# Early parking of x, a wider gate and 36 readerless products in an attention-and-mixer kernel

## The chip, the cores and the metric

The kernel runs on one core of a Trainium2 chip. The metric is the time of one execution on the device, in microseconds; runs of the kernel before have the median 647.34 us (three runs, 647.22 to 649.98).

## The reference

```python
# 4 batches, 8 heads, 768 tokens, head dim 64; chunks of 32 tokens see 16 tokens
# to the left, 8 to the right and 8 memory tokens
scores = scale * np.matmul(q_c, k_full.transpose(0, 1, 3, 2))
a = np.exp(scores - np.max(scores, axis=-1, keepdims=True))
out[:, :, c_start:c_end] = np.matmul(a / (a.sum(-1, keepdims=True) + 1e-9), v_full)
...
x = out.transpose(0, 2, 1, 3).reshape(B, S, H * D)      # 4 x 768 x 512
u = x + (x.transpose(0, 2, 1) @ U @ V).transpose(0, 2, 1)  # U 768x32, V 32x768
return u + np.maximum(u @ w_ch1, 0.0) @ w_ch2            # w1 512x2048, w2 2048x512
```

q, k, v and the memory tokens are float32. U, V, w1 and w2 are float64 in DRAM; the kernel reads them as pairs of 32-bit integers.

## The kernel before

A batch has six x tiles of 128 tokens x 512; three of them make a block (TB = 3), two make an attention step T (0 to 2). Attention of a step: q and k are transposed on TensorE (L582, out of qn and kn) and copied out by ACT (qt, L642); L661 makes the scores; DVE takes maximum and difference (`softmax_`, L697, L698), ACT the exponential (L704); pt is transposed (L760), copied by ACT (L763) and multiplied with v (L790); DVE multiplies by the reciprocal sums and so writes x (L804).

The mixer: the float64 words are put together by `Words` in four steps, begin (L216, ACT), bits (L223, L224, DVE), low (L230, ACT) and join (L237, DVE). U and V are decoded once, each piece of w1 and w2 once, for batch 0. Products with float32 accuracy are made as three, out of high and low halves (names ending in h and l). u = x + ... is made transposed (uh, ul, L1099, L1100), hidden units in pieces f = 0 to 15 of 128 (`w1_step`, L1159, then ACT's relu hh, L1165, and DVE's hl, L1166) and `w2_step` adds them up in PSUM (L1213, L1218), after a first product with v3 and the gate tile g (L1199). `add_to_x` (L1174) adds the sums to x.

Batch 0 is done in `both_blocks`: 32 units n; units 0 to 17 alternate block 0 and block 1 for f = 0 to 8, units 18 to 24 are block 0 with f = 9 to 15, units 25 to 31 the same of block 1. Batches 1 to 3 are done in `fast`, where the weights enter through sums of quarter matrices: GpSimd makes these sums (`prepare`, L1346), DVE and ACT the turned folds tl and th (L1394, L1393). In `prepare` for p = 1 GpSimd first copies one element of tl to a tile named gate_ (L1334), so that its sums start behind that part of the fold.

x tiles live in a pool of 19 buffers ("slot") that weights in raw form, temporaries and x share. `put_by` notes that an x tile is to go to DRAM, `let_go` issues the noted stores on ACT's queue (L1144), `recall` loads x back on SP's queue (L1149).

Order: the program is written engine by engine. SP's queue, the loads of q, k, v (L563: v; vbe is the third of the three v tiles, for T = 2), U, V and weights (rw and raw, L316 and L326) among it, keeps the order of the code throughout; TensorE and GpSimd too; DVE to unit 18; ACT to unit 2 (`head.close()`), and behind that a scheduler sets the order, which may also move an instruction ahead of earlier ones. DVE's one-element memset of rw (L315) makes SP's first weight load wait for DVE's place.

`keep_clock(n)` counts products of the zero tile `busy` (128x512, bf16) that `att_ps` issues ahead of the next bank's work, without a reader. FILL gives the counts for six places; the first two have 2 each, the others none.

Of the kernel before, what the change touches and what calls it, by code (L numbers as in the profile page):

```python
# [9 lines left out]
F32 = mybir.dt.float32  # L10
F32R = mybir.dt.float32r
BF16 = mybir.dt.bfloat16
# [15 lines left out]
HEAD = {ET.Activation}  # L28
FIRST = 3000
START = 90  # L30
FILL = [2, 2, 0, 0, 0, 0]
BANKS = (
    "o0 o1 h h a a a h h a a o0 o1 a a h h o0 o1 a a h h o0 o1 a a o0 o1 a h h a a o0 a a"
)
# [2 lines left out]
HIGH = 400  # L37
LEAD = 0
LATE = 0
SPLIT = 9  # L40
# [15 lines left out]
def chunk_attn_then_mixer_kernel(  # L56
# [13 lines left out]
    nc = tc.nc  # L70
    ctx.enter_context(tc.manual_schedule(engines={mybir.EngineType.SP}))
    P = 128
# [16 lines left out]
    TB = 3  # L89
    NBLK = NT // TB  # L90
    TOK = TB * P
# [51 lines left out]
    def keep_clock(n, m=0):  # L143
        warm[0] += n
        small[0] += m

    busy = slot([P, 512], BF16, "busy")
    nc.vector.memset(busy, 0.0)
# [20 lines left out]
    for j in range(4):  # L169
        nc.gpsimd.tensor_copy(  # L170
            out=rep[32 * j:32 * j + 32],
# [966 lines left out]
    def put_by(b, t):  # L1138
        held.append((x_d[b, t], xs.pop((b, t))))

    def let_go(eng=nc.scalar):
        while held:
            to, x = held.pop(0)
            eng.dma_start(out=to, in_=x)  # L1144
# [25 lines left out]

    def add_to_x(b, t, bank, last):
        x = xs[(b, t)]
        with tc.high_priority(offset=2 * HIGH if last else 0):
            nc.vector.tensor_tensor(out=x, in0=bank, in1=x, op=ALU.add)  # L1174
        if last:
            held.append((out[b, t * P:(t + 1) * P, :], xs.pop((b, t))))
            if b == B - 1 or b == 0 and t >= TB:
                let_go(nc.sync)
        else:
            put_by(b, t)  # L1180
# [3 lines left out]
    def w2_step(b, blk, f, where, begins, ends, hh, hl):  # L1184

        if begins:
            for tt in range(TB):
                if where == 1 or where == 2 and tt == 2:
                    accs[where, tt] = ps_b.tile([P, 512], F32, name="ps_a", tag="bank")
                elif where == 2:  # L1190
                    accs[where, tt] = ps_b.tile([P, 512], F32, name="ps_h", tag="bank")
                else:
                    accs[where, tt] = ps_o.tile([P, CH], F32, name=f"acc{tt}")
        acc = [accs[where, tt] for tt in range(TB)]
        if begins and f == 0 and b == 0:
            begins = False
            for tt in range(TB):
                t = blk * TB + tt
                nc.tensor.matmul(out=acc[tt], lhsT=v3[:, t * P:(t + 1) * P], rhs=gate[0], start=True, stop=False)  # L1199
        passes = [(hh, w2h[f]), (hh, w2l[f]), (hl, w2h[f])]  # L1200
        if ends is not None and b >= CLASSIC:
            for tt in range(TB):
                sl = slice(tt * P, (tt + 1) * P)
                for m, (h, w) in enumerate(passes):
                    nc.tensor.matmul(  # L1205
                        out=acc[tt], lhsT=h[:, sl], rhs=w, start=False, stop=(m == 2),
                    )
                add_to_x(b, blk * TB + tt, acc[tt], ends)
            return
        for tt in range(TB):  # L1210
            sl = slice(tt * P, (tt + 1) * P)
            for m, (h, w) in enumerate(passes[:2]):
                nc.tensor.matmul(  # L1213
                    out=acc[tt], lhsT=h[:, sl], rhs=w, start=(begins and m == 0), stop=False,
                )
        for tt in range(TB):
            sl = slice(tt * P, (tt + 1) * P)
            nc.tensor.matmul(out=acc[tt], lhsT=hl[:, sl], rhs=w2h[f], start=False, stop=ends is not None)  # L1218
        if ends is not None:
            for tt in range(TB):  # L1220
                add_to_x(b, blk * TB + tt, acc[tt], ends)
# [5 lines left out]
    def both_blocks(following):  # L1227

        units = []
        for f in range(SPLIT + LEAD):  # L1230
            if f < SPLIT:
                units.append((0, f, 0, f == 0, None))
            if f >= LEAD:
                g = f - LEAD
                units.append((1, g, 1, g == 0, False if g == SPLIT - 1 else None))
        units += [(0, f, 0, False, True if f == NF - 1 else None) for f in range(SPLIT, NF)]
        units += [(1, f, 0, f == SPLIT, True if f == NF - 1 else None) for f in range(SPLIT, NF)]
        prev = []
        for n, (blk, f, where, begins, ends) in enumerate(units):
            while done[0] < min(2 * NF, 2 * f + 1 + (n > LATE)):  # L1240
                advance(1)
                more_w()
            if n == 2:
                head.close()
            let_go()
            solo = n >= 2 * SPLIT
            if n == 2 * SPLIT:
                paced.close()
            for blk_, m, *_ in units[n:n + AHEAD + 1]:
                if m >= SPLIT and blk_ == 1:  # L1250
                    get_w1l(m)
            w1l = w1ls[f]
            if f >= SPLIT or blk == 1:
                del w1ls[f]
            if n == 2 * SPLIT - SOON:
                place(1)
            serve(RATEL if n < 2 * SPLIT else RATES)
            if n > 2 * SPLIT:
                border()
            if n == 0:  # L1260
                for c, g3 in rest[:2]:
                    join_uT1(turn_x1(c), c, g3)
            if n == len(units) - 1:
                for m in range(3):
                    build_factor(0, m)
            hid_ = w1_step(0, blk, f, w1l)
            if n == len(units) - 5:
                open_turned()
            if n == len(units) - 1:
                open_fast()  # L1270
            if n == 0:
                decode(2, 4)
                for c, g3 in rest[2:]:
                    join_uT1(turn_x1(c), c, g3)
                decode(1, 1)
                decode(2, 6)
                decode(1, 6)
                decode(3, 2)
            for _ in range(RATE + (3 < n < 12)):
                advance(1)  # L1280
                more_w()
            if n > 2 * SPLIT:
                border()
            if n == len(units) - 3:
                prepare(0, True)
            if n >= len(units) - 3:
                following()
            if n == len(units) - 1:
                recall(0, 1)
                for m in (3, 4):  # L1290
                    build_factor(0, m)
            prev.append((blk, f, where, begins, ends) + hid_)
            if solo or n % 2 == 0 or ends:
                while len(prev) > (not ends):
                    while done[0] < 2 * prev[0][1] + 2:
                        advance(1)
                        more_w()
                    w2_step(0, *prev.pop(0))
# [21 lines left out]
        place(PLAN[at[0]])  # L1320
        at[0] += 1

    gate_ = const.tile([P, 1], F32, name="gate")
    sums_d = [[dram.tile([P, 2, 2, P], F32, name=f"sumsd{p}_{m}") for m in range(3)] for p in range(NF // 2)]

    def prepare(p, first):

        if first:
            whole = [slot([P, NCK, P], F32, "val") for _ in range(2)]
            for side in range(2):  # L1330
                nc.gpsimd.dma_start(out=whole[side], in_=val_d[2 * p + side])
            mixed[p, 1], mixed[p, 3] = whole[1][:, 2:4, :], whole[0][:, 0:2, :]
            if p == 1:
                nc.gpsimd.tensor_copy(out=gate_[0:1], in_=turned[0][1][0:1, 4, 0, TOK - 1:TOK].bitcast(F32))  # L1334
        else:
            plain = slot([P, 2, 2, P], F32, "plain")
        for m, (n, fa, ca, fb, cb, op) in enumerate(SUMS):
            if m % 2 == 0:
                two = slot([P, 2, 2, P], F32, "sums")
                used = slice(0, 1 if m + 1 == len(SUMS) else 2)  # L1340
                if not first:
                    nc.sync.dma_start(out=two[:, used], in_=sums_d[p][m // 2][:, used])
            mixed[p, n] = two[:, m % 2]
            if first:
                a, b_ = (whole[f][:, 2 * c:2 * c + 2, :] for f, c in ((fa, ca), (fb, cb)))
                nc.gpsimd.tensor_tensor(out=two[:, m % 2], in0=a, in1=b_, op=getattr(ALU, op))  # L1346
                if m % 2 == 1 or m + 1 == len(SUMS):
                    summed.append((p, sums_d[p][m // 2][:, used], two[:, used]))
            elif m == 0:
                for n, side in ((1, 1), (3, 0)):  # L1350
                    mixed[p, n] = plain[:, side]
                    nc.sync.dma_start(out=plain[:, side], in_=val_d[2 * p + side][:, 2 * side:2 * side + 2])
# [244 lines left out]
```

## Time and profile before

| | |
|---|---|
| median of the runs shown | 647.34 us (647.22, 647.34, 649.98) |
| the profiled execution's own time | 647.76 us |
| its span in the profile | 646.0 us |
| granted TensorE clock, mean over the span | 0.993 of full speed |
| TensorE, DVE, ACT, GpSimd busy | 626.6, 422.4, 306.6, 75.0 us |
| chain that ended last | 88% TensorE, 4% DVE, 2% SP's queue, 2% ACT, 2% DMA |

The span is what the profiler sees, from the first to the last instruction; the execution's own time has the launch around it. Times in the rows are microseconds from the span's start. "[0.86 <-ACT dec L230]" at a row's end says that the engine was idle that long before the row's first instruction, and what ended it. Instructions of one line are merged in the timelines (x4: four of them; start and total time). Queue rows (SPq, ACTq) show the issue of a transfer, not the transfer.

### The profile page before, as it was taken

How to read it: one execution, taken by the hardware profiler on the slowest of the kernel's cores; microseconds unless marked ns; L12 is line 12 of the kernel's file. 1: busy time of each engine (PE TensorE's matmuls, PEld its weight loads, DVE VectorE, ACT ScalarE, POOL GpSimd, SP SyncE). 2: the span in 40 equal slices, each digit the busy share in tenths (PEclk: the TensorE clock that was granted, in tenths of full speed). 3: DMA queues.
4: the chain of work that ended last, by engine and by line, in shares of the span. 5: the costliest groups of instructions: out<-in, count | busy, mean ns of one | idle time of the engine just before them, and what ended most of it. 6: DMA issues, size and time to landing. Idle time of an engine off the chain costs nothing.

```text
span 646.0 us, 15746 instructions
## 1 busy us (share of the span) xinstructions
PE 626.6 (97%) x6196; PEld 548.8 (85%) x6198; DVE 422.4 (65%) x889; ACT 306.6 (47%) x770; POOL 75.0 (12%) x129
## 2 busy tenths in 40 slices
PE   7798999999999999989999999999999999999997
PEld 6567999988879899879898899888888899889986
DVE  4977997887529867449676864556666974427442
ACT  4666776685316454524344555633333653315320
POOL 3710011100120642123300000000000000000000
PEclk9999999999999999989999999999999999999999
DMA  9998695696606689414371699144532662100021
GB/s 206 192 306 294 212 261 180 181 255 177 185 22 220 183 219 208 132 35 157 100 236 52 170 208 230 43 116 124 148 114 82 189 221 90 50 34 16 2 79 69
DMA packets 134357, 96.83 MB, mean 150 GB/s; under 512 B 88842, under 2 KB 111114, under 8 KB 134282
## 3 DMA queue, kind: packets, MB, share of 16 engines
q1 hardware_dynamic: 121690, 70.25, 41.2%
q10 hardware_dynamic: 9936, 17.04, 7.2%
q0 software_dynamic: 2656, 8.52, 3.8%
q8 instruction: 49, 0.80, 0.5%
q14 instruction: 26, 0.21, 0.1%
HBM read 69.44 MB, written 25.43 MB: 147 GB/s over the span
## 4 chain that ended last, share of the span: by engine, by line
PE 88%; DVE 4%; SPq 2%; ACT 2%; DMA 2%; issue 1%; DVEq 0%; ACTq 0%
PE ps_h L1459 19%; PE acc L1213 14%; PE ps_h L1159 10%; PE ps_a L1459 8%; PE acc L1218 7%; PE ps_h L1213 6%; PE ps_a L1213 5%; PE ps_h L1218 3%; PE ps_a L582 2%; PE ps_a L1218 2%; PE ps_a L790 2%; PE ps_a L661 2%; PE ps_h L1205 1%; PE ps_a L760 1%; PE ps_a L1379 1%
## 5 line engine op out<-in xcount | busy, mean ns | idle before, releaser
L1213 PE MATMUL acc<-w,hh 128*128 128x512 f32 x366 | 97.1, 400 | 0.9 <-DVE w L367 0.9
L1459 PE MATMUL ps_h<-th,w1l 128*128 128x384 f32 x288 | 83.3, 342 | 0.5 <-DVE part L1474 0.5
L1213 PEld LDWEIGHTS acc<-w,hh 128*128 128x128 f32 x366 | 66.9, 188 | 15.2 <-issue 1.5
L1435 DVE SCALAR_TENSOR_TENSOR hl<-kept,hh 128x384 fp32r<-128x384 f32 x48 | 26.7, 556 | 50.9 <-PE ps_a L1218 25.7
L1459 PEld LDWEIGHTS ps_h<-th,w1l 128*128 128x128 f32 x288 | 52.8, 187 | 3.7 <-issue 1.7
L1434 ACT ACTIVATE hh<-kept 128x384 fp32r<-128x384 f32 x48 | 25.5, 531 | 64.0 <-PE ps_a L1213 41.5
L1459 PE MATMUL ps_h<-th,s 128*128 128x384 f32 x192 | 53.0, 337 | 0.0
L1218 PE MATMUL acc<-w,hl 128*128 128x512 f32 x183 | 51.6, 390 | 0.0
L1459 PE MATMUL ps_h<-tl,w1l 128*128 128x384 f32 x144 | 48.5, 337 | 0.0
L1213 PE MATMUL ps_h<-w,hh 128*128 128x512 f32 x156 | 43.9, 404 | 1.8 <-issue 1.8
L1159 PE MATMUL ps_h<-uh,w1h 128*128 128x384 f32 x124 | 42.5, 348 | 0.7 <-ACT uh L1131 0.6
L1159 PE MATMUL ps_h<-ul,w1h 128*128 128x384 f32 x124 | 40.9, 337 | 0.0
L1218 PEld LDWEIGHTS acc<-w,hl 128*128 128x128 f32 x183 | 34.4, 188 | 7.4
L1213 PE MATMUL ps_a<-w,hh 128*128 128x512 f32 x132 | 38.1, 392 | 1.7 <-ACT hh L1165 1.7
L1465 ACT COPY part<-ps_h 128x384 f32<-128x384 f32 x24 | 11.5, 479 | 55.5 <-PE ps_h L1459 34.5
L1427 ACT CAST s<-sums 128x256 fp32r<-128x256 f32 x72 | 28.6, 411 | 16.3 <-PE ps_h L1459 16.1
L1213 PEld LDWEIGHTS ps_h<-w,hh 128*128 128x128 f32 x156 | 29.0, 192 | 7.8 <-issue 1.9
L1459 PEld LDWEIGHTS ps_h<-th,s 128*128 128x128 f32 x192 | 35.1, 188 | 0.2 <-DVE part L1469 0.2
L1346 POOL TENSOR_TENSOR sums<-val 128x256 f32<-128x256 f32 x40 | 31.9, 825 | 28.1 <-DMA val<-vald 11.0
L1459 PE MATMUL ps_h<-tl,s 128*128 128x384 f32 x96 | 32.3, 337 | 0.0
L1213 PEld LDWEIGHTS ps_a<-w,hh 128*128 128x128 f32 x132 | 25.0, 190 | 7.5 <-ACT hh L1165 2.2
L1428 DVE TENSOR_TENSOR s<-sums,s 128x256 fp32r<-128x256 f32 x72 | 30.4, 434 | 1.0 <-ACT s L1427 0.8
(280 smaller groups left out, 1393.8 us busy)
## 6 DMA issues: line engine op xcount, KB each, us to landing
sums<-sumsd SPq DMA_DIRECT2D x32, 256.0 KB
xd<-x ACTq DMA_DIRECT2D x30, 256.0 KB
x<-xd SPq DMA_DIRECT2D x30, 256.0 KB
rw<-in_moe_w_ch_dram SPq DMA_DIRECT2D x14, 512.0 KB
vb<-in_v_dram SPq DMA_DIRECT2D x56, 98.0 KB
raw<-in_moe_w_ch_dram SPq DMA_DIRECT2D x20, 256.0 KB
qn<-in_q_dram SPq DMA_DIRECT2D x36, 128.0 KB
rw<-in_moe_w_ch_dram SPq DMA_DIRECT2D x16, 256.0 KB
```

The source lines that it names most:

```text
L582: nc.tensor.transpose(out=psv[:, p, r, :], in_=half[:, r, 2 * p:2 * p + 2, :].rearrange("n h d -> n (h d)"), identity=ident,)
L661: nc.tensor.matmul(out=psv[s][CK * i:CK * i + CK, t, p % 2, p // 2, :], lhsT=qt[p // 2][rows, p % 2, NI * t + i, :], rhs=kall[rows, NB * ( ...
L790: nc.tensor.matmul(out=psv[g][CK * i:CK * i + CK, t, j], lhsT=pt[j % 2][rows, 2 * t + j // 2, CK * i:CK * i + CK], rhs=vt[rows, NI * t + i ...
L1159: nc.tensor.matmul(out=ph[:, :TOK], lhsT=w[:, c, :], rhs=u[c], start=(m == 0), stop=(m + 1 == len(parts)),)
L1213: nc.tensor.matmul(out=acc[tt], lhsT=h[:, sl], rhs=w, start=(begins and m == 0), stop=False,)
L1218: nc.tensor.matmul(out=acc[tt], lhsT=hl[:, sl], rhs=w2h[f], start=False, stop=ends is not None)
L1346: nc.gpsimd.tensor_tensor(out=two[:, m % 2], in0=a, in1=b_, op=getattr(ALU, op))
L1427: nc.scalar.copy(out=s[:, 0:2], in_=total)
L1428: nc.vector.tensor_tensor(out=s[:, 2:4], in0=total, in1=s[:, 0:2].bitcast(F32), op=ALU.subtract)
L1434: nc.scalar.activation(out=hh, in_=src, func=AF.Relu)
L1435: nc.vector.scalar_tensor_tensor(out=hl, in0=src, scalar=0.0, in1=hh.bitcast(F32), op0=ALU.max, op1=ALU.subtract,)
L1459: nc.tensor.matmul(out=banks[at_], lhsT=w[:, wc, :], rhs=t[:, i, c, :], start=(n < 3 and m == 0), stop=(m + 1 == len(parts)), skip_group_c ...
```

## The change

- FILL[3] goes from 0 to 6: six readerless products ahead of the transposes of the last q part (`keep_clock(FILL[3])`, L911).
- `fill`: 30 readerless 32x64 products out of ident into acc[0], ahead of the gate products (L1199) of block 1's first `w2_step`; none for block 0.
- At unit 2, behind `head.close()`, x of block 0 (three tiles of 256 KB) is put by, to DRAM; at unit 21 `recall(0, 0)` loads it.
- gate_ has seven columns: GpSimd's copy reads one element of all seven parts of tl, not of part 4 alone.
- In batch 0, the last add to x has a high priority only for block 0.

```diff
-FILL = [2, 2, 0, 0, 0, 0]
+FILL = [2, 2, 0, 6, 0, 0]
...
+    def fill(ps, n):
+
+        ones = ident.bitcast(BF16)
+        for _ in range(n):
+            nc.tensor.matmul(out=ps[0:32, 0:64], lhsT=ones[:, 0:32], rhs=ones[:, 0:64], start=True, stop=True)
...
     def add_to_x(b, t, bank, last):
         x = xs[(b, t)]
-        with tc.high_priority(offset=2 * HIGH if last else 0):
+        with tc.high_priority(offset=2 * HIGH if last and (b > 0 or t < TB) else 0):
...
         if begins and f == 0 and b == 0:
             begins = False
+            fill(acc[0], 30 * blk)
             for tt in range(TB):
...
             if n == 2:
                 head.close()
+                for t in range(TB):
+                    put_by(0, t)
+            if n == 2 * SPLIT + 3:
+                recall(0, 0)
             let_go()
...
-    gate_ = const.tile([P, 1], F32, name="gate")
+    gate_ = const.tile([P, 7], F32, name="gate")
...
             if p == 1:
-                nc.gpsimd.tensor_copy(out=gate_[0:1], in_=turned[0][1][0:1, 4, 0, TOK - 1:TOK].bitcast(F32))
+                nc.gpsimd.tensor_copy(out=gate_[0:1], in_=turned[0][1][0:1, :, 0, TOK - 1].bitcast(F32))
```

ACT's queue in the kernel before, at the q copies of T = 2 (dec is U and V in decoding, qt the copied q, v_96 the tile v3); what an instruction waits for stands in brackets, DMAHW0 to DMAHW7 are the completion counters that the DMAs of SP and ACT take in turn:

```order
L216 ACTIVATE dec_749<-vraw_108 96x256 [waits DMAHW4_49,DMAHW3_49,DMAHW5_49,DMAHW1_49,DVE_49]
L642 COPY qt_756<-ps_h_751 128x2x128 [waits PE_49]
L642 COPY qt_756<-ps_h_751 128x2x128
L642 COPY qt_764<-ps_h_759 128x2x128 [waits PE_49,Activation_49]
L642 COPY qt_764<-ps_h_759 128x2x128
L763 COPY pt_625<-acc0_775 128x512 [waits PE_49]
L763 COPY pt_649<-acc1_781 128x512 [waits PE_49]
L230 ACTIVATE dec_733<-uarea_107 128x192 [waits DVE_49,Activation_49]
L230 ACTIVATE dec_749<-vraw_108 96x256 [waits DVE_49,Activation_49]
L704 ACTIVATE pt_862<-pt_862 128x512 [waits DVE_49]
L704 ACTIVATE pt_868<-pt_868 128x512 [waits DVE_49]
L265 CAST v3_96<-ps_a_956 96x256 [waits PE_49]
```

The same place of ACT's queue in the changed kernel (its lines stand some six higher):

```order
L222 ACTIVATE dec_749<-vraw_108 96x256 [waits DMAHW4_49,DMAHW3_49,DMAHW5_49,DMAHW1_49,DVE_49]
L1150 DMA xd0_0_141<-x_773 128x512 [waits DMAHW0_49,DVE_49]
L648 COPY qt_762<-ps_h_751 128x2x128 [waits PE_49]
L648 COPY qt_762<-ps_h_751 128x2x128
L1150 DMA xd0_1_142<-x_776 128x512 [waits DMAHW1_49,DVE_49]
L648 COPY qt_770<-ps_h_765 128x2x128 [waits PE_49,Activation_49]
L648 COPY qt_770<-ps_h_765 128x2x128
L769 COPY pt_625<-acc0_781 128x512 [waits PE_49]
L769 COPY pt_649<-acc1_787 128x512 [waits PE_49]
L236 ACTIVATE dec_733<-uarea_107 128x192 [waits DVE_49,Activation_49]
L1150 DMA xd0_2_143<-x_956 128x512 [waits DMAHW1_49,DVE_49]
L271 CAST v3_96<-ps_a_962 96x256 [waits PE_49]
```

The three stores of x stand in ACT's front now, the first two between the decode of V and the second pair of q copies, the third ahead of the casts of v3; between L236 and the third store there are also the second L236 and the two exponentials, as before.

SP's queue in the changed kernel, the loads of vbe, and the first weight loads behind them (this piece of the queue has the same transfers in both kernels):

```order
L569 DMA vbe_101<-in_v_dram 56x7x64 [waits DMAHW6_49,Pool_49]
L569 DMA vbe_101<-in_v_dram 56x7x64 [waits DMAHW7_49]
L569 DMA vbe_101<-in_v_dram 56x7x64 [waits DMAHW0_49]
L569 DMA vbe_101<-in_v_dram 56x7x64 [waits DMAHW1_49]
L577 DMA vbe_101<-in_v_dram 48x4x64 [waits DMAHW2_49]
...
L322 DMA rw1_879<-in_moe_w_ch1_dram 128x2x256 [waits DMAHW2_49,DVE_49]
L322 DMA raw_882<-in_moe_w_ch1_dram 128x2x256 [waits DMAHW3_49]
L332 DMA rw2_884<-in_moe_w_ch2_dram 128x1024 [waits DMAHW4_49]
```

The third load of vbe has counter 0, the fourth counter 1; the two stores of x take these counters next. The first weight load had counter 0 in the kernel before and has counter 2 now.

## Rows read from the trace of the kernel before

**Rows 1.** The page: busy time, share of the span and instructions of the engines.

```profile
PE 626.6 (97%) x6196; PEld 548.8 (85%) x6198; DVE 422.4 (65%) x889; ACT 306.6 (47%) x770; POOL 75.0 (12%) x129
```

**Rows 2.** Windows: stretch and length, each engine's busy us (instructions), clock, DMA share, GB/s.

```profile
30.00:35.00 5.00, 5.00 (x106) 3.12 (x102) 4.70 (x16) 3.19 (x7) 2.96 (x6) 0.66 0.65 148
60.00:65.00 5.00, 5.00 (x29) 4.80 (x28) 4.87 (x9) 3.35 (x7) 0.54 (x1) 1.00 0.57 215
279.00:283.00 4.00, 4.00 (x12) 3.13 (x11) 1.75 (x3) 1.56 (x3) 1.85 (x3) 0.57 0.03 7
```

**Rows 3.** Waits of TensorE: line, releaser: total us, times, longest.

```profile
PE ps_h L582 <- DVE qn L530: 1.4, 1, 1.4
PE ps_a L1459 <- DVE tl L1394: 1.0, 1, 1.0
```

**Rows 4.** Timeline of TensorE: start, total us, line, operation, count, wait before.

```profile
25.58 1.81 PE L661 MATMUL ps_a<-kall,qt 64*32 64x64 f32 x128
...
29.67 1.72 PE L790 MATMUL acc<-vb,pt 64*32 64x64 f32 x94 [1.25 <-DMA vb<-in_v_dram]
...
33.89 1.06 PE L821 MATMUL acc<-x,u_sb 128*32 128x512 f32 x8
...
58.86 1.66 PE L1213 MATMUL ps_a<-w,hh 128*128 128x512 f32 x6 [1.74 <-ACT hh L1165]
...
277.74 1.20 PE L1213 MATMUL ps_h<-w,hh 128*128 128x512 f32 x4 [1.78 <-issue]
```

**Rows 5.** Timeline of SP's queue (issues), 21 to 58 us.

```profile
21.50 5.55 SPq L563 DMA_DIRECT2D vb<-in_v_dram  x8
27.15 2.64 SPq L563 DMA_DIRECT2D vbe<-in_v_dram  x4
...
33.82 0.39 SPq L316 DMA_DIRECT2D rw<-in_moe_w_ch_dram  x1
...
51.85 0.37 SPq L316 DMA_DIRECT2D rw<-in_moe_w_ch_dram  x1
57.94 0.37 SPq L316 DMA_DIRECT2D raw<-in_moe_w_ch_dram  x1
```

**Rows 6.** Timeline of ACT, 24 to 38 us.

```profile
24.74 0.45 ACT L216 ACTIVATE dec<-vraw 96x256 f32<-96x256 f32 x1 [0.79 <-DMA vraw<-in_moe_V_dram]
25.09 1.21 ACT L642 COPY qt<-ps_h 128x256 f32<-128x256 f32 x4
...
27.10 0.41 ACT L230 ACTIVATE dec<-uarea 128x192 int32<-128x192 uint32 x1
...
32.52 0.37 ACT L265 CAST v<-ps_a 96x256 fp32r<-96x256 f32 x1 [0.40 <-PE ps_h L261]
...
37.15 0.43 ACT L216 ACTIVATE dec<-rw 128x256 f32<-128x256 f32 x1 [1.52 <-DMA rw<-in_moe_w_ch_dram]
```

**Rows 7.** Waits of SP's queue from 20 to 60 us.

```profile
SPq L316 <- ACT vbe L230: 4.8, 1, 4.8
```

**Rows 8.** Timeline of DVE, 27 to 34 us.

```profile
27.55 0.74 DVE L237 CUSTOM_DVE_ANT_0 dec<-dec 128x384 uint16<-128x384 uint16 x2 [0.86 <-ACT dec L230]
...
31.40 0.06 DVE L315 MEMSET rw<- 1x1 f32 x1
...
32.33 1.42 DVE L804 TENSOR_TENSOR x<-acc,rs 128x256 f32<-128x256 f32 x4
```

**Rows 9.** Readerless products of before: L139 in the timeline, L137 by line (ns: min/median/max).

```profile
1.47 4.87 PE L139 MATMUL acc<-busy 128*32 128x64 bf16 x90 [1.47 <-DVE kall L168]
...
L137 PE MATMUL ps_h<-busy x1: 389/389/389, 10.3 to 10.3; 128*128 128x512 bf16 x1
```

**Rows 10.** Timelines of DVE and GpSimd in the last fold, 211 to 218 us.

```profile
211.63 1.02 DVE L1394 TENSOR_TENSOR tl<-fold,th 128x512 fp32r<-128x512 f32 x2
...
213.76 2.23 DVE L1394 TENSOR_TENSOR tl<-fold,th 128x512 fp32r<-128x512 f32 x2
...
212.71 0.18 POOL L1334 COPY gate<-tl 1x1 f32<-1x1 f32 x1 [7.77 <-DVE tl L1394]
212.89 4.63 POOL L1346 TENSOR_TENSOR sums<-val 128x256 f32<-128x256 f32 x5
```

## The prediction

> **What bounds the kernel now.** I read the page's busy times first, then TensorE's waits, then the timelines of ACT, SP, PE and DVE around the places that the change touches. TensorE is busy for 97% of the span [rows 1], and from 60 us on without a break (5.00 us busy in the 5 us from 60 [rows 2]); a delay that reaches that point goes to the end whole, and a microsecond saved elsewhere counts only if TensorE waited for it. Its waits are short, and four of them meet an edit: 1.4 us for qn of the last q part, 1.74 us for hh before block 1's first w2 products, 1.0 us for tl in the last fold, and 1.78 us that end with "issue" at 277.74 [rows 3, 4]. Before 60 us the work is a relay without slack: ACT, DVE and TensorE wait for each other in turn, and DVE is busy 4.70 of the 5 us from 30 [rows 2].
>
> The profiled execution took 647.76 us around its span of 646.0; the median of the runs is 647.34. I make the sum as differences and add them to the median. 0.5% of it is 3.2 us, about what a measurement of this kernel can tell from no change.
>
> **The three stores, the large term.** They are written at unit 2, but the order puts them on ACT's queue much earlier: the first between dec<-vraw and the first two qt copies, the second between the two pairs of qt copies, the third ahead of the casts of v. Each waits for two things: the x tile, and a completion counter. The DMAs of SP and ACT take eight such counters in turn, and a DMA waits until the one before it on its counter has landed. Counted along the program, the predecessor of the first store is the third load of vbe on SP's queue, of the second store the fourth.
>
> When do these land? The eight loads of vb ahead of them are issued from 21.50 to 27.05, and the four of vbe from 27.15 to 29.79, 0.66 us each [rows 5], so the third's issue ends at about 29.1 and the fourth's at 29.8. From issue to landing: TensorE's last wait for vb ends at 29.67 [rows 4], 2.6 us after the last vb issue. So the two land at about 31.7 and 32.4. The lower bound is that they land as their issue ends. The upper is the first weight load's way, issued by 34.21 [rows 5] and waited for by ACT until 37.15 [rows 6], 2.9 us.
>
> In the kernel before, ACT copies qt at 25.09, the four in 1.21 us, to 26.30 [rows 6]. Now it stands from 25.2 to 31.7, issues, copies two, stands until 32.4, issues (0.4 us, as SP's issue of a weight load [rows 5]), and copies the other two (0.6) until 33.4: **+7.1 us** (+4.5 if landing comes with the end of issue, +7.5 at the upper bound). That ACT stands behind a waiting DMA is taken from SP, where one DMA waited 4.8 us for a decode [rows 7]: after the issue at 51.85 the next came at 57.94, and everything behind it later still [rows 5].
>
> What is queued behind: on ACT the copies of pt, L230 at 27.10 and the exponentials [rows 6]. DVE's join of the U and V words waits for that L230 (0.86 us already), and DVE's order puts the softmax of T=2, the one-element memset of rw and the second batch of x behind it: 27.55, 31.40 and 32.33 become 34.7, 38.5 and 39.4 [rows 8]. SP's first weight load waits for that memset, which no longer comes early: 33.82 [rows 5] becomes 38.5, +4.7. TensorE's scores (25.58) go to 32.8, and its 1.25 us wait for vb disappears in the hole [rows 4], but the products with x from 33.89 need DVE's x, so they too come 7.1 later. The third store then holds ACT until x is written, 0.7 us into 32.33+7.1, plus an issue: the cast of v at 32.52 [rows 6] goes to 40.5, +8.0, of which the next DVE work, already 7.1 late, feels some **0.2** (0 to 0.9).
>
> From there to 60 us nothing shortens the shift: the weights come only 4.7 us later, so every user finds them sooner than before. Two of the three 256 KB stores are on their way by 33 us; the third stands beside the weight loads and delays them by less than a load's whole way (2.9 us, as above) against 2.4 us of slack (7.1 - 4.7): 0, at most 0.5. The three loads that bring x back stand on SP's queue at about 140 us, ahead of a store of w1 that nobody waits for at once; 0 (up to 1.2, three issues).
>
> **The readerless products.** Six of 128x512 last at most 6 x 0.39 us [rows 9] against a wait of 1.4 [rows 3]; up to 0.9 us over, but qt is held until 31.7 anyway: 0. Without the hold it would be that 0 to 0.9. Thirty of 32x64 cost 14 ns each by the scores (128 in 1.81 [rows 4]) to 54 ns by the products at the start (90 in 4.87 [rows 9]), 0.4 to 1.6 us, inside a wait of 1.74 [rows 4]: 0.
>
> **The gate on all parts.** GpSimd copied the gate at 212.71 and ran its five sums beside DVE's last tl pair, which took 2.23 us where the pair before took 1.02; the sums took 4.63 us [rows 10]. Now the sums start behind the pair, at about 215. The first tl of that pair then ends 0.55 us sooner, inside TensorE's 1.0 us wait [rows 3]: **-0.5** (0 to -1.0). GpSimd's later work comes 2 us later, with waits of its own to take it.
>
> **The priority of block 1's add to x** moves nothing that the order shows: 0.
>
> **The stop at 277.74** ("issue", 1.78 us [rows 4]) has no releaser, and after it the clock is at its low level for a while: 0.57 granted over four microseconds [rows 2], which costs 4 x 0.43 = 1.7 us of products at full speed. 72 products and weight loads more ahead of it may move or remove it: likeliest it stays (0), else up to -3.5.
>
> Sum: 647.34 + 7.1 + 0.2 - 0.5 = **654.1 us**. Its own range runs from 650.6 (early landing, or the stop gone) to 656.
>
> **Rivals.**
> *The queue is not held* (the counters' waits are over by 25 us, or ACT goes on past a waiting DMA). Then qt loses at most an issue and the overrun of the six products: 647.34 - 0.5 + (0 to 1.0) = **647.1**. For it: no row of before shows a landing of these loads or a store amid ACT's front. Against it: SP's own behaviour [rows 5, 7], and issue times after 25 us [rows 5]. By the Trainium skill, "TensorE: Matmul & The Clock Gate", section "Architectural detail", ACT's instruction queue is strictly first in, first out; by that this rival holds only if the counters are there early. No run here shows it for ACT yet. Chance 0.12.
>
> *Partly absorbed*: TensorE's waits between 33 and 59 us take up to 3.5 us of the shift, if they were due to weights and not to the relay: **650.5**. Against it: 1.74 of them end on ACT [rows 4]. Chance 0.08.
>
> *A colder front*: after standing from 25.6, where the scores start now, to 32.8 TensorE resumes at 1.2 GHz and, fed in pieces, stays there to about 45 instead of returning to 2.4 GHz; in the kernel before, the hole that ends at 29.67 [rows 4] was followed by 0.66 granted from 30 to 35 [rows 2]. The products on x and the attention products between 33.89 and 45 would cost some 2 us more: **656.1**. The same page of the skill, section "HAM oscillation", describes a kernel that waits for DMAs between groups of products and begins every group at the low clock; by it the front would cost those 2 us on top of the sum. The clock of 30 to 35 agrees as to the drop; nothing here shows it repeated. Chance 0.10.
>
> *Faster*: the hold does not occur and the stop at 277.74 goes with its cold stretch, worth 1.8 + 1.7 us: 647.34 - 0.5 - 3.5 = **643.3**. It decides if TensorE runs on behind 276 us without a hole. For: the stop follows no data. Against: it needs the first rival too. Chance 0.08.
>
> **Numbers.** The forecast has 0.62. Slower by over 0.5% (above 650.6): 0.62 + 0.10 + half of the partly absorbed = 0.76. Within: 0.12 + 0.04 = 0.16. Faster: 0.08. The range must take in the unheld queue: 646.5 to 656.5 leaves out the faster case and a colder front beyond its price. The forecast alone: 650.6 to 656.
>
> **What would show it.** Right: on ACT a hole from 25.2 to about 31.7, ended by a DMA xd, with qt behind it; TensorE's scores near 33, DVE's memset of rw near 38.5, SP's first weight load there, hh for block 1's first w2 products near 66. TensorE's wait for tl at 215 is half as long, and GpSimd's gate near 215. Wrong: qt at 25 to 26, or the distance from before to after shrinking between 34 and 60 us.

## The result

The changed kernel is slower: 655.12 us in the median of six runs (653.92 to 655.32), the kernel before 648.65 us in the median of six beside it; the ratio of the two is 1.0094, with a 95% interval of 1.0066 to 1.0121, so +6.1 us (4.3 to 7.8). The forecast was 654.1, or +6.8 us. The profiled execution took 654.97 us around a span of 653.2, 7.2 more than the profiled one before. The kernel before scatters more than its first three runs showed: in the runs beside the experiments it lay between 645.2 and 653.5 us.

**Where the time went, by TensorE.** The same product stands 6.4 us later at the scores (25.58 in [rows 4], now 31.99), 7.3 at the products with x (33.89, now 41.21), 8.1 at block 1's first w2 products (58.86, now 66.95). Timeline of TensorE in the changed kernel (start, total us, line, operation, count, wait before):

```profile
22.78 1.47 PE L137 MATMUL ps_h<-busy 128*128 128x512 bf16 x6
...
31.99 2.23 PE L667 MATMUL ps_a<-kall,qt 64*32 64x64 f32 x127 [5.99 <-ACT qt L648]
...
36.87 1.55 PE L796 MATMUL acc<-vb,pt 64*32 64x64 f32 x88 [1.91 <-issue]
...
41.21 1.07 PE L827 MATMUL acc<-x,u_sb 128*32 128x512 f32 x8
...
49.53 0.55 PE L1092 MATMUL acc<-ident,x 128*128 128x128 f32 x3 [1.98 <-issue]
...
64.43 1.05 PE L151 MATMUL ps_a<-ident 128*32 128x64 bf16 x30
...
66.95 1.67 PE L1220 MATMUL ps_a<-w,hh 128*128 128x512 f32 x6 [0.60 <-ACT hh L1171]
...
149.52 1.07 PE L667 MATMUL ps_a<-kall,qt 64*32 64x64 f32 x64 [2.69 <-issue]
...
153.25 1.05 PE L1165 MATMUL ps_h<-uh,w1l 128*128 128x384 f32 x4
...
225.66 0.44 PE L1470 MATMUL ps_a<-tl,w1l 128*128 128x384 f32 x1 [0.60 <-DVE tl L1405]
...
286.45 1.19 PE L1220 MATMUL ps_h<-w,hh 128*128 128x512 f32 x4
...
307.48 0.34 PE L1470 MATMUL ps_a<-tl,s 128*128 128x384 f32 x1 [1.17 <-issue]
```

Two places of the kernel before stand here that the prediction did not use, the scores of the next batch and the products behind them (timeline of TensorE, kernel before):

```profile
139.83 0.96 PE L661 MATMUL ps_a<-kall,qt 64*32 64x64 f32 x64 [1.07 <-issue]
...
142.21 0.86 PE L1159 MATMUL ps_h<-uh,w1l 128*128 128x384 f32 x4
```

So the shift grows once more near 150 us, from 8.1 to 11.0 (142.21 to 153.25): the wait before the scores is 2.69 instead of 1.07, and behind it the clock is at its low level. It shrinks at 286.45, where the stop of 1.78 us at 277.74 [rows 4] and its slow stretch are missing: 7.1 are left at 296.45 (289.34 before). A stop of 1.17 us at 307.48, which the kernel before does not have there, belongs to a rise to 7.7 by 408.06 (400.36 before), and a short wait that is missing near 406 us takes 0.7 back. TensorE's last products come 7.0 later, and the span is 7.2 longer.

**The hole on ACT.** Timeline of ACT, changed kernel (ACTq: a transfer's issue on ACT's queue):

```profile
25.23 0.45 ACT L222 ACTIVATE dec<-vraw 96x256 f32<-96x256 f32 x1 [0.43 <-DMA vraw<-in_moe_V_dram]
31.17 0.34 ACTq L1150 DMA_DIRECT2D xd<-x  x1
31.56 0.38 ACT L648 COPY qt<-ps_h 128x256 f32<-128x256 f32 x1 [5.88 <-DMA vbe<-in_v_dram]
...
31.83 0.95 ACT L648 COPY qt<-ps_h 128x256 f32<-128x256 f32 x3
...
39.60 0.34 ACTq L1150 DMA_DIRECT2D xd<-x  x1
39.98 0.37 ACT L271 CAST v<-ps_a 96x256 fp32r<-96x256 f32 x1 [1.38 <-DVE x L810]
```

After the decode of V, ACT does nothing for 5.88 us, and what ends it is a load of vbe: the row to compare with is qt at 25.09 in [rows 6]. The store is issued at 31.17 and only then are the q copies made. The store waits for two things, its x tile and its counter. DVE had written x by 25.42 (24.02 and 1.40 us, below) and stood idle itself from 26.77 on, so only the counter is left. What hung on the q copies, first on SP's queue in the changed kernel:

```profile
27.12 1.87 SPq L569 DMA_DIRECT2D vbe<-in_v_dram  x4
...
37.98 0.39 SPq L322 DMA_DIRECT2D rw<-in_moe_w_ch_dram  x1
```

and in the timeline of DVE, with the last tl pair of the fold:

```profile
24.02 1.40 DVE L810 TENSOR_TENSOR x<-ps_a,rs 128x256 f32<-128x256 f32 x4
...
34.05 0.71 DVE L243 CUSTOM_DVE_ANT_0 dec<-dec 128x384 uint16<-128x384 uint16 x2 [7.28 <-ACT dec L236]
...
37.87 0.06 DVE L321 MEMSET rw<- 1x1 f32 x1
...
38.81 1.42 DVE L810 TENSOR_TENSOR x<-acc,rs 128x256 f32<-128x256 f32 x4
...
224.92 1.29 DVE L1405 TENSOR_TENSOR tl<-fold,th 128x512 fp32r<-128x512 f32 x2
```

The join, the memset and the second batch of x come 6.5 us later each (27.55, 31.40 and 32.33 in [rows 8]), the first weight load 4.2 (33.82 in [rows 5]). Windows of the changed kernel (stretch, length, busy us of TensorE, its weight loads, DVE, ACT, GpSimd, granted clock, DMA share, GB/s) show the clock low for longer than before in the front ([rows 2] has 0.66 from 30 to 35), and low again behind the wait at 149:

```profile
30.00:35.00 5.00, 2.97 (x168) 2.67 (x168) 0.83 (x4) 2.75 (x8) 0.53 (x1) 0.58 0.82 225
40.00:45.00 5.00, 5.00 (x151) 3.36 (x149) 2.87 (x11) 3.17 (x8) 0.32 (x1) 0.90 0.96 310
70.00:75.00 5.00, 5.00 (x29) 4.73 (x28) 4.86 (x10) 4.55 (x10) 0.54 (x1) 1.00 0.27 93
150.00:154.00 4.00, 4.00 (x59) 3.80 (x38) 2.54 (x5) 1.31 (x4) 0.18 (x1) 0.57 1.15 290
```

GpSimd in the changed kernel, to be read against [rows 10]: the copy of the gate starts behind DVE's last pair of tl, and that pair takes 1.29 us where it took 2.23; the sums take 4.08 where they took 4.63:

```profile
226.28 0.18 POOL L1345 COPY gate<-tl 1x7 f32<-1x7 f32 x1 [10.18 <-DVE tl L1405]
226.46 4.08 POOL L1357 TENSOR_TENSOR sums<-val 128x256 f32<-128x256 f32 x5
```

### The profile page after: what moved, and what is told of

The parts are those of the page before. It is cut to its first block, busy times and chain, and to the rows that moved or that the text cites. A ratio compares the mean times of both kernels' runs of the same rounds, so it can differ in the third digit from the quotient of the medians.

```text
span 653.2 us, 15844 instructions
## 1 busy us (share of the span) xinstructions
PE 628.5 (96%) x6234; PEld 551.5 (84%) x6234; DVE 423.1 (65%) x889; ACT 306.2 (47%) x770; POOL 74.6 (11%) x129
## 4 chain that ended last, share of the span: by engine, by line
PE 91%; DMA 4%; issue 2%; DVE 1%; ACT 1%; SPq 1%; ACTq 0%
PE ps_h L1470 19%; PE acc L1220 14%; PE ps_h L1165 10%; PE ps_a L1470 8%; PE acc L1225 7%; PE ps_h L1220 6%; PE ps_a L1220 5%; PE ps_h L1225 3%; PE ps_a L588 2%; PE ps_a L667 2%; PE ps_a L1225 2%; PE ps_a L796 2%; PE ps_a L766 2%; PE ps_h L1212 1%; DMA rw<-in_moe_w_ch_dram 1%
## 5 line engine op out<-in xcount | busy, mean ns | idle before, releaser
L1445 ACT ACTIVATE hh<-kept 128x384 fp32r<-128x384 f32 x48 | 25.5, 531 | 60.8 <-PE ps_a L1220 38.1
L1439 DVE TENSOR_TENSOR s<-sums,s 128x256 fp32r<-128x256 f32 x72 | 32.0, 457 | 0.9 <-ACT s L1438 0.8
L1171 ACT ACTIVATE hh<-ps_h 128x384 fp32r<-128x384 f32 x31 | 15.1, 490 | 33.4 <-PE ps_h L1165 33.4
```

Source lines behind the costliest of these rows:

```text
L1171: nc.scalar.activation(out=hh, in_=ph[:, :TOK], func=AF.Relu)
L1439: nc.vector.tensor_tensor(out=s[:, 2:4], in0=total, in1=s[:, 0:2].bitcast(F32), op=ALU.subtract)
L1445: nc.scalar.activation(out=hh, in_=src, func=AF.Relu)
```

## The experiments

The theories: 1, ACT's queue stands behind each early store until the transfer before it on its completion counter has landed; 2, the 30 products change the order on ACT near 147 us and so lengthen a wait there; 3, the stop at 277.74 varies between executions; 4, the six products move another such stop. A stop is here a wait of TensorE that the profile puts down to "issue": it names nothing that the engine waited for. The ratios below are to the kernel before, run beside each.

**The stores alone.** Diff against the kernel before:

```diff
                 head.close()
+                for t in range(TB):
+                    put_by(0, t)
+            if n == 2 * SPLIT + 3:
+                recall(0, 0)
```

> Only the three stores of x at unit 2 and their loads at unit 21; no readerless products, gate and priority as before. Theory 1 (ACT's queue stands behind the stores until the third and fourth load of vbe have landed): a hole on ACT of some 6 us that ends near 31.2, DVE's join 6.5 us later than before, TensorE 7.2 us late by 42 us; the stop of 1.8 us at 277.7 stays with its slow stretch (it moves with the rest to about 285), TensorE's wait before the scores of the next batch near 147 stays near 1.1 us; in all +7 to +8 us, about 655. Rival A (the delay comes from the other edits or from all together): the same hole missing or under 2 us, and under +2 us. Rival B (the loads and stores of x cost by their bytes): a delay that shows near 140 us, not before 42.

Measured: 652.66 us, ratio 1.0067 (1.0043 to 1.0091), so +4.3 us. Timeline of ACT:

```profile
31.65 0.35 ACTq L1150 DMA_DIRECT2D xd<-x  x1
32.04 0.66 ACT L648 COPY qt<-ps_h 128x256 f32<-128x256 f32 x2 [5.10 <-DMA vbe<-in_v_dram]
```

and of TensorE:

```profile
66.28 1.66 PE L1219 MATMUL ps_a<-w,hh 128*128 128x512 f32 x6 [1.74 <-ACT hh L1171]
```

The hole is there with the stores alone, and TensorE's program is that of the kernel before. In this trace TensorE is 7.4 us late at block 1's first w2 products (66.28) and stays so to 277 us, where the stop lasts 0.40 us instead of 1.78 and no slow stretch follows, although not one instruction of TensorE was changed: 4.5 us are left at the end. Rivals A and B fall. The total came out under the expected 7 to 8. In this trace it is the shorter stop; for the medians it is also that the profile before has an early front (the kernel before again, below).

**The stores at their place in the code.** Diff against the changed kernel:

```diff
             if n == 2:
-                head.close()
                 for t in range(TB):
                     put_by(0, t)
+                let_go()
+                head.close()
```

> The whole change, but the three stores are issued ahead of head.close(), so that they stand on ACT's queue at unit 2 itself (between the decode of w2 and a relu) and not in the front. Same bytes, same queue. Theory 1: no hole on ACT at 25 us, the scores start near 25.6, TensorE is under 1 us late by 60 us; the 3.0 us near 147 and the -3.5 us of the vanished stop at 277 stay if they belong to the other edits: 647 to 648.5. Rival B (bytes): still some +3 us or more against the kernel before.

Measured: 649.78 us, ratio 1.0029 (1.0008 to 1.0050), so +1.9 us (0.5 to 3.2). Timeline of ACT:

```profile
25.51 1.19 ACT L648 COPY qt<-ps_h 128x256 f32<-128x256 f32 x4
...
62.99 0.34 ACTq L1150 DMA_DIRECT2D xd<-x  x1
```

and of TensorE:

```profile
59.31 1.66 PE L1220 MATMUL ps_a<-w,hh 128*128 128x512 f32 x6 [0.60 <-ACT hh L1171]
```

The q copies are back at 25.51, and TensorE is 0.45 us late at block 1's first w2 products. The same bytes on the same queue at 63 us are without the hole. The median is 1.3 us over the expected range; its ten runs lie between 646.9 and 653.0.

**No stores.** Diff against the changed kernel:

```diff
                 head.close()
-                for t in range(TB):
-                    put_by(0, t)
-            if n == 2 * SPLIT + 3:
-                recall(0, 0)
```

> The whole change without the stores of x and their loads. Theory 1: as the run with the late stores, 647 to 648.5, because the bytes cost nothing; if it is over 1 us faster than that run, the stores and loads cost that much where they stand. ACT's order near 130 to 150 us is the changed one, so the wait before the next batch's scores is 2 to 3 us (1.07 before).

Measured: 648.69 us, ratio 1.0005 (0.9983 to 1.0026). The rest of the change is worth nothing that can be measured. Against the run with the late stores the medians differ by 1.1 us, but the intervals overlap: whether the stores and loads cost about a microsecond in themselves stays open. TensorE's wait before the next batch's scores was 2.8 us, as expected.

**One column of x in the stores.** The stores of the first experiment, cut to 512 bytes each, and no load (x stays where it is); diff against the kernel before:

```diff
+                for t in range(TB):
+                    held.append((x_d[0, t][:, 0:1], xs[(0, t)][:, 0:1]))
```

> The kernel before with stores of one column of the three x tiles (512 bytes in all partitions together instead of 256 KB) at the same three places of ACT's queue, with the same counters for the first two; nothing is loaded back, x stays in its buffers. Theory 1 (the wait on a counter holds the queue): the same hole on ACT, from 25.2 to about 31.2, TensorE 7 us late by 42 us, as in the run with the whole stores. Rival (what costs is the transfer of 256 KB each, or the buffers given up): no hole, under +1 us.

Measured: 652.81 us, ratio 1.0092 (1.0063 to 1.0121). Timeline of ACT:

```profile
30.54 0.38 ACTq L1150 DMA_DIRECT2D xd<-x  x1
30.96 0.38 ACT L648 COPY qt<-ps_h 128x256 f32<-128x256 f32 x1 [6.15 <-DMA vbe<-in_v_dram]
```

A store of a five-hundredth of the size costs no less than the whole one (the intervals of the two runs overlap). It is the wait in the queue, not the transfer, not the buffers that x gives up. And the hold ends with the load that the counter stood for: in the four profiles with early stores the first store is issued 2.5 to 3.0 us after the issue of the third vbe load has ended (that was at 28.50 in the changed kernel, at 29.20, 27.59 and 28.81 in the others).

**The third store alone.** With the first two gone, the third takes another counter, and so another load to wait for; diff against the kernel before:

```diff
+                put_by(0, 2)
+            if n == 2 * SPLIT + 3:
+                x = xs[0, 2] = slot([P, CH], F32, "x")
+                nc.sync.dma_start(out=x, in_=x_d[0, 2])
```

> Only the third store (and its load): ahead of the casts of v3, behind the q copies; as the first of the three it now takes counter 7, whose last taker is the tenth load of vbe, issued by SP from 33.29 to 33.72 in the kernel before. Theory 1: no hole at 25 us, the scores start near 25.6; ACT stands at the casts of v3 until that load has landed, 2.6 us after its issue, at about 36.3 (32.5 before), TensorE some 3 to 4 us late by 60 us: about 651 to 652. Rival (only a store ahead of the q copies can cost): the cast of v3 within 1 us of 32.5 and no change of the time.

Measured: 649.78 us, ratio 1.0015 (0.9995 to 1.0035), so +1.0 us (-0.3 to 2.3) instead of 3 to 4. Timeline of ACT:

```profile
26.00 1.23 ACT L648 COPY qt<-ps_h 128x256 f32<-128x256 f32 x4
...
34.84 0.35 ACTq L1150 DMA_DIRECT2D xd<-x  x1
35.23 0.37 ACT L271 CAST v<-ps_a 96x256 fp32r<-96x256 f32 x1 [2.18 <-PE ps_a L766]
```

and of SP's queue, the last load of vbe:

```profile
32.53 0.43 SPq L577 DMA_DIRECT2D vbe<-in_v_dram  x1
```

and of DVE, the writing of x:

```profile
33.26 1.42 DVE L810 TENSOR_TENSOR x<-acc,rs 128x256 f32<-128x256 f32 x4
```

The store does wait: it goes 1.9 us after the issue of vbe's last load ends at 32.96, and the cast of v behind it is made at 35.23 (32.52 in [rows 6]). But the x tile that it stores, the first two of the four pieces, was itself ready only at about 34.0 (an estimate, half of the 1.42 us), so at most 0.9 us of the wait are the counter's. TensorE was 1.0 us later in this execution already (34.93 for the products with x, 33.89 before), and the attention products of T = 2 come only 1.3 us later (36.68, 35.37 before), so it felt some 0.3 of the hold. Theory 1 fits the wait, though this run alone would not prove it, and the expectation was wrong about the price: what stands behind the third store on ACT has slack.

**The thirty products alone.** Diff against the kernel before (`fill` as in the change):

```diff
             begins = False
+            fill(acc[0], 30 * blk)
             for tt in range(TB):
```

> Only the 30 products of 32x64 ahead of block 1's first w2 products. They stand in a wait of 1.74 us and take 1.05 us in the changed kernel, so by themselves 0. But with them the scheduler sets ACT's and DVE's orders otherwise near 126 to 150 us (a cast of w1h and the decode of the last w2 piece ahead of the q copies). Theory 2 (this order makes TensorE's wait before the next batch's scores longer, and the clock fall behind it): wait 2 to 3 us near 140 (1.07 before), up to +3.0 us by 145; the stop at 277.7 may go, because 60 more instructions stand ahead of it on TensorE: -3.5 us if so; in all -0.5 to +3. Rival (that wait grows because of the stores or the shift): wait near 1.1 us and no loss near 140.

Measured: 648.61 us, ratio 0.9994 (0.9978 to 1.0011). Timeline of TensorE:

```profile
143.27 0.95 PE L667 MATMUL ps_a<-kall,qt 64*32 64x64 f32 x64 [2.80 <-issue]
...
145.30 0.52 PE L1165 MATMUL ps_h<-uh,w1h 128*128 128x384 f32 x1
```

**All but the thirty products.** Diff against the changed kernel:

```diff
             begins = False
-            fill(acc[0], 30 * blk)
             for tt in range(TB):
```

> The whole change without the 30 products of 32x64. Theory 2 (their order on ACT near 130 to 150 us costs 3 us there): TensorE's wait before the next batch's scores near 147 is 1.1 to 1.3 us, not 2.7, without the half clock behind it; 3 us less than the changed kernel by 155 us; the hole of ACT in the front stays: about 652 to 653. Rival (the wait belongs to the delayed front): 2.5 us and more stay, about 655.

Measured: 653.12 us, ratio 1.0064 (1.0039 to 1.0089). Timeline of TensorE:

```profile
67.20 1.76 PE L1219 MATMUL ps_a<-w,hh 128*128 128x512 f32 x6 [1.74 <-ACT hh L1171]
...
70.04 0.52 PE L1165 MATMUL ps_h<-uh,w1h 128*128 128x384 f32 x1
...
149.70 0.96 PE L667 MATMUL ps_a<-kall,qt 64*32 64x64 f32 x64 [1.09 <-issue]
...
150.87 0.34 PE L1165 MATMUL ps_h<-ul,w1h 128*128 128x384 f32 x1
```

With the products, alone or in the change, the wait before the next batch's scores is 2.7 to 2.8 us and the products behind it take 0.52 us, at the low clock; without them 1.09 and 0.34. Theory 2 holds for the wait: the 30 products make it longer. The page names no releaser for it ("issue"); in ACT's order a cast of w1h now stands ahead of the q copies there, and a decode pair and the cast of the last w2 piece, which stood earlier, right ahead of them. That this order is the cause, and not something else that the 30 products bring, was not separated. There is another side, though: without them the clock fell in this trace behind the wait of 1.74 us for hh (0.52 us for a product at 70.04), which cost 1.5 us by 72 us. That is seen in three of nine profiles without the 30 products, and in none of four with them (1.00 from 70 to 75 above), too few to be sure that it is no chance. If it is none, the products buy back a part of what their order costs; alone they change the time by nothing that can be measured.

**The six products alone.** Diff against the kernel before:

```diff
-FILL = [2, 2, 0, 0, 0, 0]
+FILL = [2, 2, 0, 6, 0, 0]
```

> Only the six products of 128x512 in the wait before the last q transposes. They take 1.5 us (changed kernel) in a wait that was 1.4 to 2.1 us in the runs so far: 0 there. Theory 4 (twelve more instructions, six products and six weight loads, ahead on TensorE move the point where it stands with "issue"): a stop of 1.4 to 2.0 us before the transposes of x into acc at 40 to 42 us, as in all three runs that have the six products and in none without; of it 0.3 to 1.2 us remain by 60 us, in place of the wait for g of 0.8: 0 to +1 in all. Rival (that stop comes from the stores or the shift): no stop there.

Measured: 648.47 us, ratio 1.0004 (0.9979 to 1.0029). Timeline of TensorE:

```profile
44.31 0.55 PE L1092 MATMUL acc<-ident,x 128*128 128x128 f32 x3 [1.71 <-issue]
...
279.55 0.31 PE L667 MATMUL ps_a<-kall,qt 64*32 64x64 f32 x6 [0.68 <-issue]
```

The first stop stands there with the six products, with stores or without (1.4 to 2.0 us in all five profiles that have them), and not in the profiles without. It takes the place of the wait for g, and 0.5 us remained of it in this trace by block 1's first w2 products (25.5 us behind the products with x, 25.0 before). A cost that the runs' times do not resolve, but the traces do.

**The kernel before again.** No edit.

> The kernel before, unchanged, a second profile. Theory 3 (the stop of 1.8 us at 277.7 comes from how TensorE's instructions are brought in beside other transfers, not from the program's own order): it may be there or not, with the slow stretch behind it or without; the waits of the front differ by up to 2 us between two executions. Rival (the stop belongs to the kernel before and is removed by the change): it stands at the same place with 1.8 us.

Measured: 646.4 us, one run. Timeline of TensorE:

```profile
31.10 1.18 PE L790 MATMUL acc<-vb,pt 64*32 64x64 f32 x82 [1.35 <-issue]
...
35.21 1.06 PE L821 MATMUL acc<-x,u_sb 128*32 128x512 f32 x8
...
60.07 1.66 PE L1213 MATMUL ps_a<-w,hh 128*128 128x512 f32 x6 [1.77 <-ACT hh L1165]
...
278.12 1.20 PE L1213 MATMUL ps_h<-w,hh 128*128 128x512 f32 x4 [1.06 <-issue]
...
280.31 1.07 PE L1213 MATMUL ps_h<-w,hh 128*128 128x512 f32 x4
```

The stop is there with 1.06 us instead of 1.78, and the four products behind it take 1.07, at full speed (1.91 in the profile before). 2.4 us of the profile that the prediction was made from were that execution's own. Theory 3 holds for the size of the stop. Its place does go with the readerless products: in all seven profiles without them it stands ahead of these same products (0.40 to 1.78 us), in the two with the six and not the thirty it stands in the scores just ahead of them, six products and six weight loads earlier (279.55 in the run above), and in none of the four with the thirty does it stand here; three of those have one of 0.67 to 1.17 us some 20 us later (307.48 in the changed kernel).

The front of this execution says something else that the prediction could not know. The products with x come 1.3 us later than in the first profile and block 1's first w2 products 1.2 us, so against this profile the changed kernel is 6.0 and 6.9 us late there, not 7.3 and 8.1. In the nine profiles without an early store ACT's q copies start at 25.09 to 27.77 us (26.26 here, the middle one), in the four with it at 30.96 to 32.04. The profile that the prediction was made from is the earliest of the nine.

**The gate alone, twice.** Diff against the kernel before:

```diff
-    gate_ = const.tile([P, 1], F32, name="gate")
+    gate_ = const.tile([P, 7], F32, name="gate")
...
-in_=turned[0][1][0:1, 4, 0, TOK - 1:TOK].bitcast(F32))
+in_=turned[0][1][0:1, :, 0, TOK - 1].bitcast(F32))
```

> Only the gate on all seven parts. GpSimd's gate copy 2 us later, DVE's last pair of tl in 1.3 us instead of 2.23, TensorE's wait for tl 0.6 us instead of 1.0: -0.4 us, which the measurement cannot tell from nothing (ratio 0.998 to 1.002). Rival (the later sums hold up what follows, or the changed order of the sums' stores on ACT costs): a new wait of TensorE between 215 and 260 us and over +1 us.

> The gate alone once more, in more runs, since it came out faster than the kernel before by more than its 0.4 us: if the first result holds, ratio 0.995 to 0.999; if that was chance, 0.998 to 1.002.

Measured: 645.53 us, ratio 0.9972 (0.9950 to 0.9994); again, 647.45 us, ratio 0.9981 (0.9959 to 1.0004). TensorE's wait for tl is 0.6 us, as expected, and a short wait for a part near 406 us is gone too (0.23 us, some 0.6 until the products behind it). That makes 1 us; the medians say 0.8 to 2.5. That the gate removes this wait is not shown: the profile with the thirty products alone lacks it as well. The second ratio lies in both of the expected ranges, so it does not say whether the first was chance. It is the only part of the change that leans to the faster side, and the fastest version here, by less than 0.5%.

## Why the prediction was right, and where its terms were not

| term | forecast | traces, against the first profile |
|---|---|---|
| the stores, to the products with x | +7.3 | +7.3 (33.89 to 41.21) |
| six products, to block 1's first w2 products | 0 | +0.8 (8.1 at 66.95) |
| thirty products, to 153 us | 0 | +2.9 (11.0 at 153.25) |
| the gate, to the last fold | -0.5 | -0.3 |
| the stop at 277.74 | 0, else up to -3.5 | -3.6 (7.1 at 296.45) |
| from there to 408 us, a stop at 307.48 in it | 0 | +0.6 |
| from there to the end, a wait near 406 us missing | 0 | -0.7 |
| sum | +6.8 | +7.0 (span 7.2) |

- **The hold of ACT's queue**: right in kind and place, shown by the stores alone, by their one-column form and by their later place. Its size was 0.6 us lower on ACT and DVE (6.5 instead of 7.1): SP issued the four vbe loads in 1.87 us, not 2.64, so the third's issue ended near 28.5; the 2.6 us from there to landing (31.17) agree. TensorE is 0.8 later than that, behind a stop of 1.91 us at 36.87, where the first profile had a wait of 1.25 for vb, and transposes at the low clock. So the +7.3 is met by luck in part: a smaller hold, an addition that was not foreseen, and a first profile with an early front; against the second one the products with x are 6.0 late.
- **The relay without slack to 60 us**: right. TensorE's shift at the products with x (7.3 us) is still there at 66.95 (8.1), although the weights came only 4.2 us later.
- **The third store**: ACT's cast of v came at 39.98 (40.5 forecast), and behind it DVE felt 0.1 us (0.2 forecast): right. In the run with this store alone DVE waited 0.95 us for that cast and TensorE felt 0.3.
- **The rival "not held"**: shown wrong. The Trainium skill ("TensorE: Matmul & The Clock Gate", section "Architectural detail") has ACT's instructions strictly first in, first out; the hole of 5.88 us agrees.
- **The colder front**: half of it happened. The clock stayed low to about 41 us (0.58 from 30 to 35, 0.90 from 40 to 45), but of the 2 us at most 0.8 came, TensorE's extra above; that the rest was hidden because most of the work there had DVE to wait for is argued, not shown.
- **The readerless products at 0**: the step that failed. Their own time was hidden as forecast (1.47 and 1.05 us), but the step looked at the place where they stand, not at what they move elsewhere: the six carry a stop to 49.53, and with the thirty ACT's order is another some 85 us later, where TensorE's wait grows from 1.07 us to 2.7. The prediction had TensorE without a break from 60 us on, from one window; its own trace has that wait of 1.07 us at 139.83, and no term looked at it.
- **The stop at 277.74**: taken as likeliest staying, with up to -3.5 if the readerless products move or remove it. They did move it, and its size also varies in the kernel before itself. The two misses, +3.7 and -3.6, cancelled by luck; the total is closer than its parts.

## What to carry to other kernels

A store on ACT's queue stood there like any other instruction, and what was behind it waited: before moving one, ask which earlier transfer it has to see landed, and what stands behind it in that queue. That a scheduler puts a store at the first place where its data is ready does not make it free. And a profile is one execution: look at a second one before a stop without a releaser is booked as gain or loss, or a shift is read to a microsecond.

## What the runs showed of the hardware that was not expected

- Stops of TensorE with "issue" as their releaser, 0.4 to 2.5 us long, move with the number of its instructions (49.53 with the six products, none there without; the later one six products and six weight loads earlier) and vary between executions of one kernel (1.78 and 1.06 us at the same products). Eleven of the thirteen profiles have one of 1.2 to 2.5 us among the attention products on vb, near 31 to 37 us; the one that the prediction was made from has not. The page counts 49 transfers on a queue of kind "instruction"; that the stops wait for these is a guess here, not shown.
- The clock fell behind TensorE's wait of 1.74 us for hh in some executions and not in others of the same kernel; with the 30 products in that wait no profile showed it.
- DVE's pair of tl took 2.23 us beside GpSimd's sums and 1.29 without them, for the same work (2.23 or 2.24 in all seven profiles with the narrow gate, 1.28 or 1.29 in all six with the wide one).
